# Shifting where the stationary operands of a 256-wide matmul stream lie in SBUF

## The chip, the core and the metric

One core of one Trainium2 chip runs the kernel. TensorE (PE) multiplies: an instruction first loads a stationary operand (LDWEIGHTS, the row PEld of the profile), then streams a moving operand through it into PSUM (MATMUL). VectorE is DVE, ScalarE is ACT, GpSimd is POOL, and SP issues DMAs. SBUF has 128 partitions; "byte" below means a byte within each partition. The metric is the device time of one execution, in microseconds (us).

## The reference

Linear attention with an RMS norm, followed by a feed-forward layer with GELU, all in fp32:

```
kv  = einsum('bhsd,bhse->bhde', k, v)            # q, k, v: 8 x 8 heads x 576 x 64
o   = einsum('bhsd,bhde->bhse', q, kv)
x   = o / sqrt(mean(o*o, -1) + 1e-6) * g_norm    # as 4608 tokens x 512
h   = x @ w_in                                   # 512 x 2048
out = gelu(h) @ w_out                            # 2048 x 512
```

## The kernel before

The 4608 tokens are handled in nine chunks of 512 (`CH`). Precision comes from splitting each fp32 operand into a high part in the fp32r format and the rest, so that one product is three matmuls: high by high, low by high, high by low. All work is recorded by hand in the order in which each engine runs it.

For the first two chunks (`PLAIN`) layer 1 is `layer1` (L529 in the profile): 128 x 128 weights stationary, 512 tokens streaming. Meanwhile the weights are loaded, split, and combined by `combine`, `high_sums` and `low_sums` into seven block sums per pair of feature blocks, written to DRAM as `products`.

For the last seven chunks layer 1 runs as a Strassen-like scheme, `layer1_pair` (L436): each of eight pairs of feature blocks takes seven products of six matmuls, 42 in all, with 256 columns streaming. The chunk has eight such pairs, so there are 7 x 8 x 42 = 2352 of these matmuls. Their stationary operand is a 128 x 128 piece (512 bytes) of a **ring** of four tiles, `w_in0` to `w_in3`, which `load_products` fills from DRAM (L419), one tile of 4096 bytes per two products, and refills as soon as its second product is issued. Their moving operand is a kilobyte of a token tile (`x0` to `x5` or `w_in5` to `w_in12`, by `piece_tile`). DVE adds (L446, L428) join the products in PSUM; ACT takes the GELU (L541, L542), DVE the low part (L547).

After each group of 42 comes layer 2, `layer2` (L555): 24 matmuls of 512 columns, with `gh`/`gl` or the tiles `w_in13`, `w_in14` stationary and `w_out` tiles moving. Between the two, now and then, stands `project` (L211): `q` times the key-value sums of the next chunk, six matmuls whose widths add up to 512 per part (a chunk of tokens may cross a batch). Its stationary operand is a 512-byte piece of `kv_h` or `kv_l`, its moving operand a piece of `qh`, `ql` or `w_in4`.

Tiles of the pool `const` lie one behind the other in SBUF in the order in which their names first occur; a name keeps its place, and the tile is used again under it. Four small constants come first, then `kv_h`, `kv_l`, `ident`, `fold`, `warm` (512 bytes of zeros for the matmuls of `keep_warm`, L638, early on), `half_g`, `heads`, and then the 4096-byte tiles.

Of the kernel before, what the change touches and what calls it, by code (L numbers as in the profile page):

```python
# [8 lines left out]
F32 = mybir.dt.float32  # L9
F32R = mybir.dt.float32r  # L10
I32 = mybir.dt.int32
# [5 lines left out]
P = 128  # L17
# [6 lines left out]
RING = 4  # L24
# [11 lines left out]
def linear_attn_rms_gelu_ffn(  # L36
# [18 lines left out]
    NT, DM = out.shape  # L55
# [5 lines left out]
    NF = w_in.shape[0]  # L61
# [4 lines left out]
    const = ctx.enter_context(tc.tile_pool(name="const", bufs=1))  # L66
# [8 lines left out]
    kv_l = [const.tile([P, NP, P], F32R, name=f"kv_l{s}") for s in range(2)]  # L75
    ident = const.tile([P, P], F32, name="ident")
    fold = const.tile([P, P], F32, name="fold")
    warm = const.tile([P, P], F32, name="warm")
    half_g = const.tile([P, 1], F32, name="half_g")
    heads = const.tile([P, 2], F32, name="heads")  # L80


    kv_in, late = {}, {}

    def late_tile(name):

        if name not in late:
            late[name] = const.tile([P, 2 * DM], I32, name=name).bitcast(F32)
        return late[name]
# [254 lines left out]
    kept = {}  # L344

    def reused(i, dtype=F32):

        if i not in kept:
            kept[i] = const.tile([P, 2 * DM], dtype, name=f"w_in{i}")
        return kept[i]  # L350

    def piece_tile(c, n):
        k = (["x2", "x3"] + [f"w_in{i}" for i in range(5, 10)],
# [40 lines left out]
    def high_sums():  # L394

        for (j, second), s in stage.items():
            if j % 2:
                t = reused(second, F32R).rearrange("p (k a n) -> p k a n", k=2, a=2)
            else:
                t = const.tile([P, 2, 2, HALF], F32R, name=f"x{2 + second}")  # L400
            nc.scalar.copy(out=t[:, :, 0], in_=s)
            halved[j, second] = s, t
        stage.clear()
# [10 lines left out]
    ring = {}  # L414

    def load_products(t):
        if t < (NCH - PLAIN) * NT2:
            ring[t] = reused(t % RING, F32R)
            nc.sync.dma_start(out=ring[t].bitcast(F32), in_=products[t % NT2])  # L419

    def layer1_pair(at, j, between):


        a, b = (ps_h.tile([P, CH], F32, name="ps_h") for _ in range(2))
        left, right = slice(0, HALF), slice(HALF, CH)
        u = reused(15).rearrange("p (a n) -> p a n", n=HALF)
        p1, u2, v, u3 = (u[:, i] for i in range(4))
        add = lambda out, x, y: nc.vector.tensor_tensor(out=out, in0=x, in1=y, op=ALU.add)  # L428

        def product(k, out, first=False):  # L430
            n = ((at.c - PLAIN) * NF // 2 + j) * NPR + k
            w, x = ring[n // 2][:, n % 2 * DM:(n % 2 + 1) * DM], at.x[k]
            for kb in range(2):
                hi, lo = (w[:, m * HALF + kb * P:m * HALF + (kb + 1) * P] for m in range(2))
                for i, (y, z) in enumerate(((hi, 0), (lo, 0), (hi, 1))):
                    nc.tensor.matmul(  # L436
                        out=out, lhsT=y, rhs=x[:, z, kb], start=first and kb + i == 0,
                        stop=kb == 1 and i == 2, skip_group_check=True,
                    )
            if n % 2:  # L440
                load_products(n // 2 + RING)
# [25 lines left out]
    raw, parts = {}, {}  # L467

    def load_w(n):
        kind, i = weights[n]  # L470
        src = w_in[i] if kind == "in" else w_out[i * P:(i + 1) * P, :]
        raw[n] = const.tile([P, 2 * DM], I32, name=f"w_{kind}{i}")
        nc.sync.dma_start(out=raw[n], in_=src.bitcast(I32))

    zs, ws = {}, {}
# [27 lines left out]

    def high_w(n):
        kind, i = weights[n]
        t = const.tile([P, 2 * DM], F32R, name=f"w_{kind}{i}")
        parts[kind, i] = t
        nc.scalar.copy(out=t[:, HI], in_=ws[n].bitcast(F32))

# [89 lines left out]

    attn = [Attn(c) for c in range(NCH)]  # L600
    first, second = attn[:2]
    nc.vector.memset(warm, 0.0)
    nc.scalar.activation(out=heads, in_=warm[:, :2], func=AF.Gelu)
    mask, g_row = late_tile(f"w_in{NF - 6}")[:, :P], late_tile(f"w_in{NF - 6}")[:1, P:2 * P]
# [12 lines left out]
    for h in range(2):  # L617
        nc.scalar.dma_start(out=g_row[:, h * D:(h + 1) * D], in_=g_norm.unsqueeze(0))
    load_w(0)
    for p in range(2):  # L620
        load_kv(1, p)
    for n in (1, 2, 3):
        load_w(n)
    for p in (2, 3):
        load_kv(1, p)
    load_w(4)
    second.load(0)
    for n in range(5, 9):
# [49 lines left out]
    n = 2 * NB  # L678
# [156 lines left out]
    def later(c, i):  # L835

        if i == 9:
            sums[c] = attn[c + 1].fold()
        if i in (5, 7):
            load_kv(c + 2, (i - 5) // 2)  # L840
        if i == 9:
            attn[c + 2].load(0)
        if i == 13:
            for p in (2, 3):
                load_kv(c + 2, p)
        if i == 15:
            attn[c + 2].load(1)
        if i == 13:
            for t in range(RING):
                load_products(t)  # L850
# [5 lines left out]
    def convert(i, gelu_rest, between):  # L856

        count = 3 if i in (2, 4, 6, 8) else 2 if i < 11 else i in (11, 12, 14)  # L860
        now = [order.pop(0) for _ in range(count)]
        for k, n in enumerate(now or [None]):
            if last:
                high_w(last[0])
                if last[0] + 2 < len(weights):
                    top_w(last[0] + 2)
            if not i and not k:
                gelu_rest()
                low_w(last.pop())
            if n is not None:  # L870
                bits_w(n)
            if i and not k:
                gelu_rest()
            if last:
                low_w(last.pop())
            if n is not None:
                last.append(n)
            if not k:
                between()
# [7 lines left out]
    for s in range(PLAIN * NF):  # L887
        c, i = divmod(s, NF)
# [7 lines left out]
        if c == 0:  # L896
# [4 lines left out]
            def between():  # L901
                if i == 0:
                    for p in (2, 3):
                        attn[0].low_x(p, nc.vector)
                if i in (9, 10):
                    high_w(i - 9)
                    low_w(i - 9)
                if i == 1:
                    split_kv(1, range(NP))
                    nc.scalar.copy(out=kv_h[0], in_=kv_f)  # L910
                    nc.vector.tensor_tensor(
                        out=kv_l[0], in0=kv_f, in1=kv_h[0].bitcast(F32), op=ALU.subtract
                    )
                spread_work(c, i)
# [9 lines left out]
        else:  # L924
# [3 lines left out]
            n = 0 if not 1 <= i <= 11 else 2 if i in (1, 3, 5, 7, 11) else 1  # L928
# [114 lines left out]
```

## Time and profile before

| | |
|---|---|
| three timed runs | 836.03, 837.2, 839.48 us; median 837.2 |
| the profiled execution | 835.6 us, of which 833.8 us are the span from first to last instruction |
| granted TensorE clock, mean | 0.999 |
| DVE, ACT, POOL busy | 59%, 38%, 8% of the span |
| TensorE rows of the first layer's products (L436) | 1392 + 960 matmuls, 283 ns each as reported |
| a ring load, issue to landing | least 3.1, median 4.6, most 9.2 us |

A reported matmul duration is from start to a modelled end, and neighbours overlap. What a matmul costs in a dense stream is the distance from its start to the next one's start, and this is read from the timeline, where the rows show starts.

### The profile page before, as it was taken

Reading aid. Unit: us, or ns where it says so; the run is one execution under the profiler, and the core shown is the slowest. Engines: PE = TensorE matmul, PEld = TensorE weight load, DVE = VectorE, ACT = ScalarE, POOL = GpSimd, SP = SyncE. Lnnn points to the kernel's source line nnn. Section 1 sums busy time; section 2 is a strip of 40 time slices with the busy share of each in tenths; the row PEclk is TensorE's granted clock in tenths of the full one; section 3 lists DMA queues with packets and bytes.
Section 4 is the critical chain, followed back from the end, with each engine's and each line's share of the span. In section 5 each row is a group of like instructions: output and inputs, shape, how many; then the busy total and the mean of one; then the engine's idle time right before and its main releaser. Section 6 shows DMA issues by size and latency. Waiting matters only on the chain.

```text
span 833.8 us, 13801 instructions
## 1 busy us (share of the span) xinstructions
PE 828.9 (99%) x5386; PEld 735.0 (88%) x5386; DVE 495.9 (59%) x980; ACT 314.2 (38%) x578; POOL 65.5 (8%) x69
## 2 busy tenths in 40 slices
PE   9999999999999999999999999999999999999998
PEld 7688888888999999999999999999999989999997
DVE  3999838687546744674457545673467446744443
ACT  3788444434532334233423253233323332322221
POOL 1000021011000101010001010010101000100000
PEclk9999999999999999999999999999999999999999
DMA  9981347776784568455945587456555655556551
GB/s 348 407 330 51 114 135 250 254 245 240 252 304 135 180 230 307 161 177 202 339 159 176 199 281 262 151 177 229 172 172 172 232 188 177 177 177 227 177 177 51
DMA packets 61605, 174.97 MB, mean 210 GB/s; under 512 B 6500, under 2 KB 15460, under 8 KB 61540
## 3 DMA queue, kind: packets, MB, share of 16 engines
q1 hardware_dynamic: 61536, 174.09, 60.0%
q8 instruction: 43, 0.70, 0.3%
q14 instruction: 22, 0.18, 0.1%
q10 hardware_dynamic: 4, 0.00, 0.0%
HBM read 149.95 MB, written 24.12 MB: 209 GB/s over the span
## 4 chain that ended last, share of the span: by engine, by line
PE 99%; DVE 0%; issue 0%; ACT 0%; DVEq 0%
PE acc L555 47%; PE ps_h L436 34%; PE ps_h L529 10%; PE ps_a L211 3%; PE ps_a L151 2%; PE ps_h L521 1%; PE ps_h L638 1%; PE acc L672 0%; PE acc L739 0%; PE ps_h L683 0%; PE ps_a L241 0%; DVE w L594 0%; DVE w_in L664 0%; PE ps_h L691 0%; DVE sq L583 0%
## 5 line engine op out<-in xcount | busy, mean ns | idle before, releaser
L555 PE MATMUL acc<-w_out,gh 128*128 128x512 f32 x700 | 217.0, 391 | 0.0
L436 PE MATMUL ps_h<-w_in,w_in 128*128 128x256 f32 x1392 | 176.2, 283 | 0.0
L436 PEld LDWEIGHTS ps_h<-w_in,w_in 128*128 128x128 f32 x1392 | 171.1, 192 | 0.0
L555 PE MATMUL acc<-w_out,w_in 128*128 128x512 f32 x672 | 159.7, 392 | 0.0
L555 PEld LDWEIGHTS acc<-w_out,gh 128*128 128x128 f32 x700 | 129.3, 188 | 25.5
L555 PEld LDWEIGHTS acc<-w_out,w_in 128*128 128x128 f32 x672 | 124.0, 188 | 24.8
L555 PE MATMUL acc<-w_out,gl 128*128 128x512 f32 x350 | 136.3, 390 | 0.0
L541 ACT ACTIVATE gh<-ps_h 128x512 fp32r<-128x512 f32 x88 | 52.7, 599 | 212.6 <-DVE ps_h L428 155.4
L436 PEld LDWEIGHTS ps_h<-x,w_in 128*128 128x128 f32 x960 | 122.6, 191 | 4.4
L436 PE MATMUL ps_h<-x,w_in 128*128 128x256 f32 x960 | 123.9, 283 | 0.0
L541 ACT ACTIVATE w_in<-ps_h 128x512 fp32r<-128x512 f32 x56 | 33.6, 600 | 184.7 <-DVE ps_h L428 184.7
L446 DVE COPY w_in<-ps_h 128x256 f32<-128x256 f32 x56 | 23.8, 425 | 133.1 <-PE ps_h L436 133.1
L428 DVE TENSOR_TENSOR ps_h<-ps_h,w_in 128x256 f32<-128x256 f32 x168 | 72.7, 432 | 48.0 <-PE ps_h L436 43.6
L428 DVE TENSOR_TENSOR w_in<-ps_h,w_in 128x256 f32<-128x256 f32 x168 | 71.4, 425 | 49.2 <-PE ps_h L436 47.2
L529 PE MATMUL ps_h<-x,w_in 128*128 128x512 f32 x360 | 86.8, 390 | 0.0
L547 DVE TENSOR_TENSOR gl<-ps_h,gh 128x512 fp32r<-128x512 f32 x88 | 60.4, 687 | 42.4 <-ACT ps_h L542 38.0
L542 ACT ACTIVATE ps_h<-ps_h 128x512 f32<-128x512 f32 x144 | 85.5, 594 | 0.0
L529 PEld LDWEIGHTS ps_h<-x,w_in 128*128 128x128 f32 x360 | 67.4, 188 | 13.9 <-POOL x L299 0.2
L555 PEld LDWEIGHTS acc<-w_out,gl 128*128 128x128 f32 x350 | 65.7, 188 | 14.1
L547 DVE TENSOR_TENSOR w_in<-ps_h,w_in 128x512 fp32r<-128x512 f32 x56 | 38.4, 686 | 17.1 <-ACT ps_h L542 17.1
L199 POOL TENSOR_TENSOR ql<-q,qh 128x512 fp32r<-128x512 f32 x16 | 21.1, 1321 | 211.5 <-ACT qh L198 140.9
L334 POOL TENSOR_TENSOR w_in<-o,w_in 128x512 fp32r<-128x512 f32 x13 | 16.9, 1325 | 210.8 <-ACT w_in L329 210.8
(153 smaller groups left out, 640.4 us busy)
## 6 DMA issues: line engine op xcount, KB each, us to landing
w_in<-products SPq DMA_DIRECT2D x196, 512.0 KB, 4.6
products<-w_in SPq DMA_DIRECT2D x40, 256.0 KB, 3.0
w_in<-w_in SPq DMA_DIRECT2D x16, 512.0 KB, 10.2
kv_main<-kv_main SPq DMA_DIRECT2D x16, 512.0 KB, 7.0
w_out<-w_out SPq DMA_DIRECT2D x16, 512.0 KB, 10.2
q<-qT SPq DMA_DIRECT2D x15, 512.0 KB, 5.7
out<-w SPq DMA_DIRECT2D x18, 256.0 KB, 2.1
out<-z SPq DMA_DIRECT2D x17, 256.0 KB, 2.3
```

Of the source, the lines that this page charges most:

```text
L151: nc.tensor.matmul(out=ps[r, n * D:(n + 1) * D], lhsT=k[:, r], rhs=v[:, r], start=(j == 0), stop=(j == NJ),)
L199: eng.tensor_tensor(out=ql, in0=q, in1=qh.bitcast(F32), op=ALU.subtract)
L211: nc.tensor.matmul(out=ps[:, a:e], lhsT=w, rhs=x[:, a:e], start=(m == 0), stop=(m == 2))
L334: eng.tensor_tensor(out=x[:, 1], in0=self.block(OPERANDS[n]), in1=x[:, 0].bitcast(F32), op=ALU.subtract,)
L428: add = lambda out, x, y: nc.vector.tensor_tensor(out=out, in0=x, in1=y, op=ALU.add)
L436: nc.tensor.matmul(out=out, lhsT=y, rhs=x[:, z, kb], start=first and kb + i == 0, stop=kb == 1 and i == 2, skip_group_check=True,)
L446: nc.vector.tensor_copy(out=p1, in_=a[:, left])
L529: nc.tensor.matmul(out=h, lhsT=parts["in", i][:, w][:, p * P:(p + 1) * P], rhs=at.x[p][:, x], start=(m + p == 0), stop=(m == 2 and p == NP ...
L541: nc.scalar.activation(out=gh, in_=h, func=AF.Gelu)
L542: nc.scalar.activation(out=h, in_=h, func=AF.Gelu)
L547: nc.vector.tensor_tensor(out=gl, in0=h, in1=gh.bitcast(F32), op=ALU.subtract)
L555: nc.tensor.matmul(out=ps, lhsT=x[:, ts], rhs=parts["out", i][:, w], start=(i == 0 and m == 0), stop=(m == 2 and (i == NF - 1 or (i, t) == ...
```

## The change

Each of the ring's four tiles `w_in0` to `w_in3` gets 64 elements (256 bytes) more, and the ring's loads and matmuls use the part that starts 48 elements (192 bytes) into the tile. Other uses of the same four tiles (the raw weights and their split parts early on, the staging tiles of `high_sums`) still start at the tile's first byte. To make room, `warm` is no longer a tile: it becomes a part of `w_in10`, which already holds other early constants.

```diff
-    warm = const.tile([P, P], F32, name="warm")
+    AWAY, ROOM = 48, 64
+
+    def block_tile(name, dtype):
+        ring = name in [f"w_in{i}" for i in range(RING)]
+        return const.tile([P, 2 * DM + (ROOM if ring else 0)], dtype, name=name)
...
-            kept[i] = const.tile([P, 2 * DM], dtype, name=f"w_in{i}")
-        return kept[i]
+            kept[i] = block_tile(f"w_in{i}", dtype)
+        return kept[i][:, :2 * DM]
...
-            ring[t] = reused(t % RING, F32R)
+            reused(t % RING, F32R)
+            ring[t] = kept[t % RING][:, AWAY:AWAY + 2 * DM]
...
-        raw[n] = const.tile([P, 2 * DM], I32, name=f"w_{kind}{i}")
+        raw[n] = block_tile(f"w_{kind}{i}", I32)[:, :2 * DM]
...
-        t = const.tile([P, 2 * DM], F32R, name=f"w_{kind}{i}")
+        t = block_tile(f"w_{kind}{i}", F32R)[:, :2 * DM]
...
+    warm = late_tile(f"w_in{NF - 6}")[:, DM + P:DM + 2 * P]
     nc.vector.memset(warm, 0.0)
```

Where the operands lie follows from the built program. The table gives the first byte of some tiles in a partition, and in brackets how far that is past a multiple of 256. Pieces within a tile start at multiples of 512 from it.

| tile | used as | before | after |
|---|---|---|---|
| `kv_h`, `kv_l` (four tiles) | stationary, L211 | 16512 to 22656 (128) | the same |
| ring part in `w_in0` | stationary, L436 | 59072 (192) | 58752 (128) |
| ring part in `w_in1` | stationary, L436 | 63168 (192) | 63104 (128) |
| ring part in `w_in2` | stationary, L436 | 71360 (192) | 71552 (128) |
| ring part in `w_in3` | stationary, L436 | 91840 (192) | 92288 (128) |
| `w_in5` | moving, L436 | 108224 (192) | 108736 (192) |
| `x2` | moving, L436 | 165568 (192) | 166080 (192) |
| `qh`, `ql` | moving, L211 | 198592, 200640 (192) | 199104, 201152 (192) |
| `gh` | stationary, L555 | 202688 (192) | 203200 (192) |
| `w_out2` | moving, L555 | 95936 (192) | 96448 (192) |

No other tile's remainder by 256 changes either, apart from the small `half_g` and `heads`. The order of the instructions is the same on every engine. One wait is new. On SP the rows around the load of `w_in10`, the tile in which `warm` now lies, were these (names carry buffer numbers; in brackets, what the instruction waits for):

```order
L473 DMA w_in_188<-w_in 128x1024 [waits DMAHW6_49]
L473 DMA w_out_190<-w_out 128x1024 [waits DMAHW7_49]
L473 DMA w_in_192<-w_in 128x1024 [waits DVE_49,DMAHW0_49,Activation_49,Pool_49]
L473 DMA w_out_194<-w_out 128x1024 [waits DMAHW1_49]
L473 DMA w_in_196<-w_in 128x1024 [waits DMAHW2_49,DVE_49,PE_49]
```

and are now these:

```order
L481 DMA w_in_187<-w_in 128x1024 [waits DMAHW6_49]
L481 DMA w_out_189<-w_out 128x1024 [waits DMAHW7_49]
L481 DMA w_in_191<-w_in 128x1024 [waits DVE_49,PE_49,DMAHW0_49,Activation_49,Pool_49]
L481 DMA w_out_193<-w_out 128x1024 [waits DMAHW1_49]
L481 DMA w_in_195<-w_in 128x1024 [waits DMAHW2_49,DVE_49,PE_49]
```

The load of `w_in10` (the third row) now waits for TensorE as well, since the early matmuls on zeros read that tile.

## The prediction

> **What bounds the kernel now.** I read the page first: busy shares, then the chain that ended last.
>
> ```profile
> PE 828.9 (99%) x5386; PEld 735.0 (88%) x5386; DVE 495.9 (59%) x980; ACT 314.2 (38%) x578; POOL 65.5 (8%) x69
> PEclk9999999999999999999999999999999999999999
> PE acc L555 47%; PE ps_h L436 34%; PE ps_h L529 10%; PE ps_a L211 3%; PE ps_a L151 2%; PE ps_h L521 1%; PE ps_h L638 1%; PE acc L672 0%; PE acc L739 0%; PE ps_h L683 0%; PE ps_a L241 0%; DVE w L594 0%; DVE w_in L664 0%; PE ps_h L691 0%; DVE sq L583 0%
> ```
>
> TensorE is busy from end to end, the clock is granted in full, and the chain is TensorE alone. The first layer's products (L436), whose stationary operand is what the change moves, hold 34% of 833.8 us, some 283 us. The view of who waited for whom, taken for PE, is two rows long:
>
> ```profile
> PE ps_h L638 <- DVE warm L602: 1.1, 1, 1.1
> PE acc L672 <- DVE w_in L664: 0.6, 2, 0.4
> ```
>
> Both are at the start. So there is no stall to remove: the change can only act on the distance from one matmul's start to the next. The page's duration of a matmul (283 ns) doesn't give that, because neighbours overlap; the timeline of PE does. It gives start, length, and how many:
>
> ```profile
> 302.30 0.39 PE L555 MATMUL acc<-w_out,gl 128*128 128x512 f32 x1
> ...
> 307.07 0.39 PE L555 MATMUL acc<-w_out,gl 128*128 128x512 f32 x1
> 307.29 3.04 PE L436 MATMUL ps_h<-x,w_in 128*128 128x256 f32 x24
> 310.17 2.32 PE L436 MATMUL ps_h<-w_in,w_in 128*128 128x256 f32 x18
> 312.33 0.28 PE L211 MATMUL ps_a<-w_in,kv_h 128*128 128x256 f32 x1
> ```
>
> Read the starts. From 307.29 to 310.17 are 24 products, from 310.17 to 312.33 are 18: 2.88/24 = 2.16/18 = **120.0 ns each**. From 302.30 to 307.07 are 21 matmuls of layer 2 (they come in threes): 4.77/21 = 227.1 ns each. Twice the columns cost 107 ns more, so about 0.42 ns is a column's time, and 120 ns is 107 ns of streaming and 13 ns of something else; 227 ns leaves the same 13 or 14 ns. The products have 2352 x 13 ns = 31 us of this. That is all there is to win, and one nanosecond per product is 2.35 us.
>
> **Does the place of the operands bear on these 13 ns?** Before, stationary and moving pieces of L436, L529 and L555 all start 192 bytes past a multiple of 256. `project` (L211) is the only stream of the same kind in which they differ: `kv` lies 128 past, `q` 192 past. That is exactly how the change places the products. In one chunk `project` is 256 columns wide, the same shape as the products:
>
> ```profile
> 301.15 0.28 PE L211 MATMUL ps_a<-qh,kv_h 128*128 128x256 f32 x1
> 301.26 0.28 PE L211 MATMUL ps_a<-qh,kv_l 128*128 128x256 f32 x1
> 301.37 0.28 PE L211 MATMUL ps_a<-ql,kv_h 128*128 128x256 f32 x1
> 301.49 0.28 PE L211 MATMUL ps_a<-qh,kv_h 128*128 128x256 f32 x1
> 301.60 0.28 PE L211 MATMUL ps_a<-qh,kv_l 128*128 128x256 f32 x1
> 301.71 0.28 PE L211 MATMUL ps_a<-ql,kv_h 128*128 128x256 f32 x1
> 301.83 0.63 PE L555 MATMUL acc<-w_out,gh 128*128 128x512 f32 x2
> ...
> 315.75 0.28 PE L211 MATMUL ps_a<-qh,kv_h 128*128 128x256 f32 x1
> ...
> 316.46 2.89 PE L555 MATMUL acc<-w_out,w_in 128*128 128x512 f32 x12
> 319.19 1.00 PE L436 MATMUL ps_h<-x,w_in 128*128 128x256 f32 x7
> ```
>
> At 301.15, right behind a group of products, six take 0.68 us: **113 ns each**, and every step is 110 or 120 ns in rows rounded to 10. At 315.75, right behind layer 2, six take 0.71 us: **118 ns**. Both are below 120.0, with the same opcode, shape, data type and clock. (Rounding leaves 2 ns either way on a mean of six, so 118 could nearly be 120; 113 could not.) Wider ones of the same stream show nothing of the sort:
>
> ```profile
> 682.03 0.39 PE L211 MATMUL ps_a<-w_in,kv_h 128*128 128x512 f32 x1
> 682.26 0.39 PE L211 MATMUL ps_a<-w_in,kv_l 128*128 128x512 f32 x1
> 682.49 0.39 PE L211 MATMUL ps_a<-w_in,kv_h 128*128 128x512 f32 x1
> 682.72 0.62 PE L555 MATMUL acc<-w_out,gh 128*128 128x512 f32 x2
> ```
>
> Three of 512 columns take 0.69 us, 230 ns each against 227 in layer 2: no gain, rather a loss of 3 ns. So the reading is narrow: with 256 columns a weight load lies beside the whole of the matmul before it, and there the place of the two operands seems to matter; with 512 it doesn't.
>
> **The change part by part.**
>
> *The shift of the ring.* After it all 2352 products have the placing of the L211 rows. The size per product is between 120.0 − 113.3 = 6.7 ns and −3 ns (the 512-wide rows). Which row is nearest? The products always follow layer 2, and the 256-wide row that follows layer 2 is the one at 315.75, with 118.3 ns. I take it: (120.0 − 118.3) x 2352 = 1.7 x 2352 = 4.0 us. That it is one group of six, and that the stream's pace depended on what ran ahead of it, are why I keep the other ends.
>
> *Leaving the stream.* Behind a group of products or of fast `project` matmuls, layer 2 needs a little longer than its own pace; the next rows show it behind another 256-wide `project` that follows products (six in 0.68 us again).
>
> ```profile
> 324.22 0.28 PE L211 MATMUL ps_a<-w_in,kv_h 128*128 128x256 f32 x1
> ...
> 324.90 0.63 PE L555 MATMUL acc<-w_out,gh 128*128 128x512 f32 x2
> ...
> 330.37 3.04 PE L436 MATMUL ps_h<-x,w_in 128*128 128x256 f32 x24
> ```
>
> 24 take 5.47 us, 20 ns more than 24 x 227.1; behind the 118 ns group, 12 take 2.73 us (316.46 to 319.19), 5 ns more than 12 x 227.1. With 56 groups of products, some 15 ns each come back: 0.8 us, say 1. Sum: 5 us.
>
> *The longer tiles.* Everything behind the ring moves by multiples of 256 bytes; layer 2's operands keep their remainders, and its 24 matmuls after each group kept the same 227 ns whether their stationary was `gh` or `w_in` (2.73/12 above is 227.5 as well), though these lie a different number of kilobytes from `w_out`. I take nothing, and bound it by 1 ns on 1722 matmuls of layer 2, 1.7 us either way.
>
> *The ring's loads* land on other bytes, as many as before.
>
> ```profile
> w_in<-products SPq DMA_DIRECT2D x196, 512.0 KB, 4.6
> DMA to landing us min/median/max: 3.1/4.6/9.2
> ```
>
> A tile is refilled while the three others serve 36 products, and a layer 2 always falls into that stretch: 36 x 0.120 + 5.45 = 9.8 us against a landing of 4.6 us (9.2 at most). Products at 113 ns leave 9.5. Cost nothing; if the cover were gone, a load late by 1 us in a few of 196 places would cost a few microseconds, and PE's waits show none now.
>
> *The faster PE* asks DVE for its sums sooner:
>
> ```profile
> 308.93 0.42 DVE L446 COPY w_in<-ps_h 128x256 f32<-128x256 f32 x1 [3.70 <-PE ps_h L436]
> 310.37 0.42 DVE L428 TENSOR_TENSOR w_in<-ps_h,w_in 128x256 f32<-128x256 f32 x1 [0.56 <-PE ps_h L436]
> ```
>
> The copy is done at 309.35, and the product that writes there again starts at 310.17; at 113 ns this slack of 0.8 us shrinks by less than 0.1. Nothing is late next: TensorE's stream is still the longest.
>
> *`warm` inside `w_in10`.* The memset, the same matmuls and the same waits. The load of `w_in10` on SP now waits for TensorE too; behind it on SP stand the other weight loads.
>
> ```profile
> 38.91 0.33 SPq L473 DMA_DIRECT2D w_in<-w_in  x1
> L638 PEld LDWEIGHTS ps_h<-warm x26: 186/333/338, 1.1 to 18.3; 128*128 128x128 f32 x26
> ```
>
> The load is issued at 38.91 us; the last matmul on zeros starts at 18.4. The wait is over 20 us before: nothing.
>
> Against the profiled execution: 835.6 − 5 = 830.6 us. The median shown is 1.6 us above that execution, so 837.2 − 5 = **832.2 us**, a ratio of 0.994.
>
> **The rivals.**
>
> *A, the full step.* The stream settles at the pace of the rows at 301.15 (113.3 ns). For: the groups at 301.15 and 324.22, both behind products, hold it for six matmuls each, the first without drifting, and 42 in a row have time to settle. Against: the only group that starts behind layer 2 as the products do held 118. Price: 6.7 x 2352 = 15.7 us; **821.5 us**.
>
> *B, no effect.* The 113 and 118 ns come from something else in `project` (its place in the stream, PSUM tile or the region where `kv` lies), and the products stay at 120 ns: **837 us**. For: the 512-wide rows gain nothing from the same placing. Against: the 42 products from 307.29 on read four ring tiles and seven token tiles in many places, always at the same remainder, and their pace is 120.0 throughout. The Trainium skill, "TensorE: Matmul & The Clock Gate", section "Part 2: What happens when you issue a matmul", says that loading the next tile's weights takes no SBUF read bandwidth from the running matmul, since the two have ports of their own; by it no address could matter and B would hold. The rows at 301.15 speak against it, though no run yet shows that the address is the reason.
>
> *C, slower.* The placing hurts where it is not accompanied by `project`'s own order: the products behave as the 512-wide `project` rows, 3.3 ns longer than streams at equal remainders. That is 3.3 x 2352 = 7.8 us; **845 us**. It decides from 1.8 ns per product on (4.2 us). Against: those rows are 512 wide, the products are not.
>
> **How the numbers follow.** My forecast (118, allowing 115.5 to 119.5) has 0.42, A (113 to 115.5) 0.28, B 0.20, C 0.10. The forecast is the likeliest, so 832.2 us. The range takes in A and B with the bound of layer 2: from 821.5 − 1 = 820.5 to 837.2 + 1.7 = 839; it leaves out most of C. Measurements of this kernel can tell a change of about 0.5%, 4.2 us. Faster by more: all of A and about three quarters of my own case, 0.60. Within: the rest of it and B, and a little of C: 0.32. Slower by more: 0.08.
>
> **What would show it.** In the timeline of the changed kernel, the 24 first products of a group behind layer 2: 2.84 us if 118, 2.72 if A, 2.88 if B, 2.96 if C. L555 stays at 227 ns, L529 as it is, PE's list of waits stays two rows, and 34% of the chain falls to about 33%. I'd be wrong if the pace depends on something that `project` has and the products don't, or if layer 2 changes its pace although its remainders are the same.

## The result, and the profile after

The changed kernel took 830.35 us (median of four runs, 829.81 to 831.25) against 838.34 us of the kernel before beside it (836.03 to 841.06): a ratio of 0.9916, 95% interval 0.989 to 0.9941. Measured once more on another occasion (e12 below) it took 830.14 us against 836.1, a ratio of 0.9924 (0.9901 to 0.9947). The forecast was 832.2 us and a ratio of 0.994.

The profiled execution of the changed kernel took 831.25 us, its span 829.5. First the page's busy shares and its chain by line (line numbers are 7 to 9 higher now: L444 is what L436 was, L563 is L555, L218 is L211):

```profile
PE 824.6 (99%) x5386; PEld 731.4 (88%) x5386; DVE 496.3 (60%) x980; ACT 314.0 (38%) x578; POOL 65.7 (8%) x69
PEclk9999999999999999999999999999999999999999
PE acc L563 47%; PE ps_h L444 33%; PE ps_h L537 10%; PE ps_a L218 3%; PE ps_a L158 3%; PE ps_h L529 1%; PE ps_h L647 1%; PE acc L681 1%; PE acc L748 0%; PE ps_h L692 0%; PE ps_a L248 0%; DVE w L602 0%; DVE w_in L673 0%; PE ps_h L700 0%; DVE sq L591 0%
```

TensorE still holds the whole chain, and the products went from 34% to 33% of it. The view of who waited for whom on PE still has two rows, both at the start:

```profile
PE ps_h L647 <- DVE w_in L611: 1.1, 1, 1.1
PE acc L681 <- DVE w_in L673: 0.6, 2, 0.4
```

So nothing new waits on TensorE, and the ring's loads land as they did (median 4.6, most 9.0 us). The timeline of PE shows the same group of products as before, and the `project` groups around it; the first column is the start:

```profile
302.14 0.63 PE L563 MATMUL acc<-w_out,gh 128*128 128x512 f32 x2
...
307.59 2.99 PE L444 MATMUL ps_h<-x,w_in 128*128 128x256 f32 x24
310.41 2.28 PE L444 MATMUL ps_h<-w_in,w_in 128*128 128x256 f32 x18
312.53 0.28 PE L218 MATMUL ps_a<-w_in,kv_h 128*128 128x256 f32 x1
...
313.24 2.89 PE L563 MATMUL acc<-w_out,w_in 128*128 128x512 f32 x12
```

From 307.59 to 312.53 are 42 products in 4.94 us, where it was 5.04: 117.6 ns each in place of 120.0. The 24 matmuls of layer 2 ahead of them take 5.45 us, 227.1 ns each, as before. And `project` behind the products (312.53 to 313.24) now takes 0.71 us for its six where it took 0.68, although the distance of its own operands is what it was: behind products at the same distance it goes on at their pace. All distances between starts added up, the 2352 products took 276.9 us in place of 281.8, and layer 2 took 393.2 in place of 393.9. That is 5.6 us. The two profiled spans differ by 4.3 us only: all other matmuls together took 1.3 us more in this execution, whose granted clock was 0.95 over its first 33 us (1.00 in the kernel before). What the medians differ by beyond 5.6 us, 6 to 8 us in all, lies within the scatter of the kernel before, whose runs reach from 835 to 841 us.

### The profile page after: what moved, and what is told of

Read it like the earlier page. It is cut to its first block, busy times and chain, and to the rows that moved or that the text cites. A ratio compares the mean times of both kernels' runs of the same rounds, so it can differ in the third digit from the quotient of the medians.

```text
span 829.5 us, 13801 instructions
## 1 busy us (share of the span) xinstructions
PE 824.6 (99%) x5386; PEld 731.4 (88%) x5386; DVE 496.3 (60%) x980; ACT 314.0 (38%) x578; POOL 65.7 (8%) x69
## 4 chain that ended last, share of the span: by engine, by line
PE 99%; DVE 0%; issue 0%; ACT 0%; DVEq 0%
PE acc L563 47%; PE ps_h L444 33%; PE ps_h L537 10%; PE ps_a L218 3%; PE ps_a L158 3%; PE ps_h L529 1%; PE ps_h L647 1%; PE acc L681 1%; PE acc L748 0%; PE ps_h L692 0%; PE ps_a L248 0%; DVE w L602 0%; DVE w_in L673 0%; PE ps_h L700 0%; DVE sq L591 0%
## 5 line engine op out<-in xcount | busy, mean ns | idle before, releaser
L563 PE MATMUL acc<-w_out,gh 128*128 128x512 f32 x700 | 216.7, 391 | 0.0
L444 PE MATMUL ps_h<-w_in,w_in 128*128 128x256 f32 x1392 | 173.0, 279 | 0.0
L444 PEld LDWEIGHTS ps_h<-w_in,w_in 128*128 128x128 f32 x1392 | 167.8, 188 | 0.0
L563 PE MATMUL acc<-w_out,w_in 128*128 128x512 f32 x672 | 159.3, 391 | 0.0
L563 PEld LDWEIGHTS acc<-w_out,gh 128*128 128x128 f32 x700 | 129.2, 188 | 25.3
L563 PEld LDWEIGHTS acc<-w_out,w_in 128*128 128x128 f32 x672 | 123.9, 188 | 24.6
L563 PE MATMUL acc<-w_out,gl 128*128 128x512 f32 x350 | 136.3, 389 | 0.0
L444 PEld LDWEIGHTS ps_h<-x,w_in 128*128 128x128 f32 x960 | 120.9, 188 | 4.3
L444 PE MATMUL ps_h<-x,w_in 128*128 128x256 f32 x960 | 122.2, 279 | 0.0
L436 DVE TENSOR_TENSOR ps_h<-ps_h,w_in 128x256 f32<-128x256 f32 x168 | 72.7, 433 | 46.1 <-PE ps_h L444 42.3
L436 DVE TENSOR_TENSOR w_in<-ps_h,w_in 128x256 f32<-128x256 f32 x168 | 71.4, 425 | 46.8 <-PE ps_h L444 44.9
L555 DVE TENSOR_TENSOR gl<-ps_h,gh 128x512 fp32r<-128x512 f32 x88 | 60.4, 687 | 43.0 <-ACT ps_h L550 38.7
L563 PEld LDWEIGHTS acc<-w_out,gl 128*128 128x128 f32 x350 | 65.7, 188 | 13.9
L555 DVE TENSOR_TENSOR w_in<-ps_h,w_in 128x512 fp32r<-128x512 f32 x56 | 38.4, 686 | 17.1 <-ACT ps_h L550 17.1
```

The costliest lines, as they stand in the source:

```text
L444: nc.tensor.matmul(out=out, lhsT=y, rhs=x[:, z, kb], start=first and kb + i == 0, stop=kb == 1 and i == 2, skip_group_check=True,)
L555: nc.vector.tensor_tensor(out=gl, in0=h, in1=gh.bitcast(F32), op=ALU.subtract)
L563: nc.tensor.matmul(out=ps, lhsT=x[:, ts], rhs=parts["out", i][:, w], start=(i == 0 and m == 0), stop=(m == 2 and (i == NF - 1 or (i, t) == ...
```

## The experiments

"Distance" below is the start of the stationary operand less that of the moving one, by its remainder in steps of 256 bytes: 0 before the change, 192 after it. Every kernel computes the whole result. A pace "from the starts" is the mean distance between the starts of neighbouring matmuls in the trace, taken by place in the group of 42; where rows can show it, they do.

### The longer tiles alone, and other shifts: e1, e2, e3

```diff
-    AWAY, ROOM = 48, 64
+    AWAY, ROOM = 0, 64      # e1; 16 in e2, 32 in e3
```

Expected of e1:

> The changed kernel with the ring's operands put back at the tiles' first byte: the longer tiles and the moved zeros stay, the shift of 192 bytes goes. Theory R (what counts is where the stationary operand lies relative to the moving one): the products are back at 120.0 ns each, 2.88 us for the 24 behind a layer 2, and the time is that of before within 0.5%. Rival G (the longer tiles or the removed tile made the gain): the products stay at 118 ns and the time stays near 830 us.

Of e2:

> The changed kernel with the shift at 64 bytes in place of 192, so that the ring's operands start at a multiple of 256, 64 bytes past the moving ones' remainder. Theory R doesn't say what 64 bytes give: 120 ns if the two streams still meet, 113 to 118 if any distance helps. Rival L (the weight load itself is faster when it starts at a multiple of 128 bytes, wherever the moving operand is): 118 ns, as with 192 bytes.

Of e3:

> The changed kernel with the shift at 128 bytes: the ring's operands start 64 bytes past a multiple of 256. Rival L (alignment of the weight load to 128 bytes): 120 ns, since the start is again 64 past a multiple of 128, as before the change. Theory R: some pace other than 120 ns is possible, 113 to 118, since the distance to the moving operand is 128.

Measured: e1 836.5 us, ratio 1.0005 (0.999 to 1.002); e2 832.26 us, 0.9945 (0.9927 to 0.9963); e3 837.71 us, 1.0021 (1.0006 to 1.0036). The timeline of PE, e1:

```profile
307.49 3.04 PE L444 MATMUL ps_h<-x,w_in 128*128 128x256 f32 x24
310.37 2.32 PE L444 MATMUL ps_h<-w_in,w_in 128*128 128x256 f32 x18
312.53 0.28 PE L218 MATMUL ps_a<-w_in,kv_h 128*128 128x256 f32 x1
```

e2:

```profile
308.15 2.99 PE L444 MATMUL ps_h<-x,w_in 128*128 128x256 f32 x24
310.98 2.29 PE L444 MATMUL ps_h<-w_in,w_in 128*128 128x256 f32 x18
313.10 0.28 PE L218 MATMUL ps_a<-w_in,kv_h 128*128 128x256 f32 x1
```

e3:

```profile
307.77 3.05 PE L444 MATMUL ps_h<-x,w_in 128*128 128x256 f32 x24
310.66 2.32 PE L444 MATMUL ps_h<-w_in,w_in 128*128 128x256 f32 x18
312.82 0.28 PE L218 MATMUL ps_a<-w_in,kv_h 128*128 128x256 f32 x1
```

42 products take 5.04 us in e1, 4.95 in e2, 5.05 in e3: 120.0, 117.9 and 120.2 ns. So the longer tiles and the moved zeros do nothing (to within 0.2%), and the shift does all of it. In e1 the ring tiles also lie elsewhere against the token tiles than in the kernel before, `w_in1` by 768 bytes, and the pace is the same 120.0: steps of 256 bytes do nothing, which is why the distance is counted by its remainder. Shifts of 64 and 192 bytes give the same pace, 0 and 128 nearly the same (e3's products took 282.7 us from the starts, against 281.8). These three kernels don't decide between theory R and rival L: starts 64 bytes past a multiple of 128 are the slow ones (the kernel before, e1, e3), starts at a multiple of 128 the fast ones (the changed kernel, e2), just as L has it. The next kernel separates the two.

### Everything moved together: e4

```diff
     heads = const.tile([P, 2], F32, name="heads")
+    pad = const.tile([P, 48], F32, name="pad")
```

> The kernel before with an unused tile of 192 bytes ahead of the large tiles, so that the ring's operands and the moving operands all start 128 bytes past a multiple of 256. Rival L (alignment of the weight load alone): the products fall to 118 ns. Theory R: the two are at the same remainder again, so the products stay at 120.0 ns; and the 256-wide products of q with the key-value sums, whose stationary operand keeps its 128 and whose moving one now has 128 too, rise from 113 and 118 to 120 ns.

One execution, 836.45 us beside a median of 836.84 for the kernel before. Its timeline of PE (L437 are the products, L212 is `project`):

```profile
307.67 3.04 PE L437 MATMUL ps_h<-x,w_in 128*128 128x256 f32 x24
310.54 2.32 PE L437 MATMUL ps_h<-w_in,w_in 128*128 128x256 f32 x18
312.70 0.28 PE L212 MATMUL ps_a<-w_in,kv_h 128*128 128x256 f32 x1
...
313.42 2.91 PE L556 MATMUL acc<-w_out,w_in 128*128 128x512 f32 x12
316.17 0.28 PE L212 MATMUL ps_a<-qh,kv_h 128*128 128x256 f32 x1
...
316.88 2.91 PE L556 MATMUL acc<-w_out,w_in 128*128 128x512 f32 x12
```

The stationary operands start where the changed kernel has them, 128 past a multiple of 256, and the products are at 120 ns (18 in 2.16 us). `project`, at distance 0 for the first time, takes 0.72 us for six behind the products, 120 ns where it was 113. With the stationary operands of both streams at remainder 128, the pace is 120 ns: at these places it is the distance between the two operands that counts, not the start of the stationary one.

One part of the expectation failed. The group of `project` behind layer 2 (316.17 to 316.88) takes 0.71 us at distance 0, just as it did at distance 192, and not 0.72. The starts show why: its steps are 113, 119 and then four of 120 ns, in sum 712; at distance 192, in the kernel before, they were 118, 118, 118, 117, 118 and 115, in sum 704. The first products of each group in the kernel before also go at 113.3, 119.1 and then 120.0 ns. Six matmuls behind layer 2 are too few to tell the two distances apart in rows rounded to 10 ns.

### Finer steps, four distances in one kernel: e5, e8

```diff
-    AWAY, ROOM = 48, 64
+    AWAY, ROOM = (8, 24, 40, 56), 64      # e5; (2, 4, 12, 52) in e8
...
-            ring[t] = kept[t % RING][:, AWAY:AWAY + 2 * DM]
+            ring[t] = kept[t % RING][:, AWAY[t % RING]:AWAY[t % RING] + 2 * DM]
```

> The changed kernel with a shift of its own for each ring tile: 32, 96, 160 and 224 bytes for w_in0 to w_in3. So far 0 and 128 bytes gave 120 ns per product, 64 and 192 gave 117.8. Theory S (steps of 64 bytes count, and what lies between goes with its neighbours): 32, 96, 160 and 224 each give between 117 and 121 ns, the same for all four, since each lies halfway. Theory T (the distance counts byte by byte and the streams meet only near 0 and 128): all four below 118.5 ns, and one of them may be at the 113 ns that the products of q held right behind products at distance 0. A tile serves twelve products in a row, so each pace is read from steps 3 to 12.

> The changed kernel with 8, 16, 48 and 208 bytes of shift for w_in0 to w_in3. Theory S (steps of 64 bytes): 8 and 16 still at 120 ns, 48 near 118, 208 at 118. Theory T (byte by byte): 8 and 16 already differ from 120 ns.

From the starts, means over the 588 products of each tile: e5 118.5, 118.6, 119.6 and 116.8 ns for 32, 96, 160 and 224 bytes; e8 116.4, 118.2, 118.3 and 116.7 ns for 8, 16, 48 and 208. Steps of 64 bytes (S) are out: 8 bytes already make a difference. That all lie below 118.5 (T) is out too: 160 bytes give 119.6. Single steps from start to start range from 112 to 125 ns within a tile, and the same place in a chunk's eight groups gives the same value to about a nanosecond in every chunk. The times of one execution each, 836.68 and 833.46 us, aren't read further: in e5 the products took 3.5 us less than before, but all other matmuls together 4.4 us more, with a granted clock of 0.90 over the first 33 us (1.00 in the kernel before).

### What runs ahead: e6 and its mirror, e11

`load_products` places each product of a tile by itself: 192 bytes in, or at distance 0 where it is the first of its group of seven.

```diff
-            ring[t] = kept[t % RING][:, AWAY:AWAY + 2 * DM]
-            nc.sync.dma_start(out=ring[t].bitcast(F32), in_=products[t % NT2])
+            at = [AWAY + DM * a if (2 * t + a) % NPR else 0 + (DM + ROOM) * a for a in range(2)]
+            ring[t] = [kept[t % RING][:, o:o + DM] for o in at]
...
-            w, x = ring[n // 2][:, n % 2 * DM:(n % 2 + 1) * DM], at.x[k]
+            w, x = ring[n // 2][n % 2], at.x[k]
```

(A tile whose halves no longer touch is loaded by two DMAs. In e11 the condition picks the last product of the group, `!= NPR - 1`.)

> The changed kernel with the first product of each group of seven (six matmuls) at distance 0 again and the other six at 192 bytes; its tile is loaded by two DMAs in place of one. In the trace of before, matmuls at 192 bytes ran at 113 ns right behind a stream at distance 0 and at 118 ns right behind layer 2. Theory M (the pace is set by how the stream is entered, and holds): the first product runs at 113, 119, 120 ns, then the other 36 at 113.3, 4.8 us per group in place of 4.95; with 56 groups some 6 to 9 us less than the changed kernel, about 822 to 825 us. Rival D (the 113 ns decay within some ten matmuls): the last products of a group are at 118, and the time is within 2 us of the changed kernel's 830.

> As the kernel with the first product of each group at distance 0, but it is the last product that is at 0; the tiles are loaded with as many DMAs. Theory M (the pace is set by how the stream is entered): the first six products are at 118 ns as in the changed kernel, the last one near 120, and the time is that of the changed kernel within 2 us, about 830. Rival Q (one product in seven at another distance, or the split loads, make the 113 ns): the six products at 192 bytes run at 113 ns here too, and the time is near 822 us.

e6 took **822.47 us**, a ratio of 0.9826 (0.9802 to 0.985) to the kernel before. Its timeline of PE:

```profile
305.69 2.92 PE L454 MATMUL ps_h<-x,w_in 128*128 128x256 f32 x24
308.45 2.20 PE L454 MATMUL ps_h<-w_in,w_in 128*128 128x256 f32 x18
310.49 0.28 PE L218 MATMUL ps_a<-w_in,kv_h 128*128 128x256 f32 x1
```

The 18 products from 308.45 on take 2.04 us: 113.3 ns each. From the starts, over all 56 groups, the first product's six go at 113.3, 119.1, 120.0, 120.0, 120.0 and 120.9 ns, and each of the next 36 at 113.3 or 113.4. The products take 268.4 us in all. e11 (one execution, 831.37 us), the same number of loads and of shifted products, only the odd one last:

```profile
306.91 2.99 PE L454 MATMUL ps_h<-x,w_in 128*128 128x256 f32 x24
309.74 2.28 PE L454 MATMUL ps_h<-w_in,w_in 128*128 128x256 f32 x18
311.86 0.28 PE L218 MATMUL ps_a<-w_in,kv_h 128*128 128x256 f32 x1
```

24 in 2.83 us, 118 ns, for operands that run at 113 ns in e6. So distance 192 has two paces, each steady over 36 matmuls, and what ran ahead decides which. I missed the last product: it stays at 118.2 ns on the mean from the starts, not near 120. Distance 0, entered from products at 192 bytes, doesn't reach 120 within six.

### Layer 2: e7

```diff
+        if p == 3:
+            work.tile([P, 48], F32, name="pad")
         sq[p] = work.tile([P, CH], F32, name=SQ[p], bufs=2 if p == 3 else None)
```

> The kernel before with an unused tile of 192 bytes ahead of gh, so that the stationary operands of those layer 2 products that use gh and gl lie 192 bytes from the moving ones' remainder, while those that use w_in13 and w_in14 stay at distance 0; the first layer's products are as before. If the gain were a matter of the two operands' distance alone, the 512-wide products would fall from 227 to some 224 ns, 1050 of them, 2 to 3 us. As I read the 512-wide products of q (229 to 230 ns), they gain nothing: 227 to 230 ns, and the time is that of before or up to 3 us more.

838.2 us, a ratio of 1.0022 (1.0005 to 1.0039). The timeline of PE:

```profile
303.06 0.39 PE L555 MATMUL acc<-w_out,gl 128*128 128x512 f32 x1
...
307.87 0.39 PE L555 MATMUL acc<-w_out,gl 128*128 128x512 f32 x1
308.10 3.04 PE L436 MATMUL ps_h<-x,w_in 128*128 128x256 f32 x24
...
313.14 0.28 PE L211 MATMUL ps_a<-w_in,kv_h 128*128 128x256 f32 x1
...
313.85 2.93 PE L555 MATMUL acc<-w_out,w_in 128*128 128x512 f32 x12
...
320.05 3.04 PE L436 MATMUL ps_h<-x,w_in 128*128 128x256 f32 x24
...
325.08 0.28 PE L211 MATMUL ps_a<-w_in,kv_h 128*128 128x256 f32 x1
...
325.76 0.62 PE L555 MATMUL acc<-w_out,gh 128*128 128x512 f32 x2
```

21 matmuls of 512 columns at distance 192 take 4.81 us, 229.0 ns, against 227.1 at distance 0. The shift that helps 256 columns costs these 512-wide ones 2 ns; all of layer 2 took 395.4 us from the starts, 1.5 us more than before.

The rows behind them show how far back the stream's history reaches. The 42 products from 308.10 on follow a layer 2 at distance 192, those from 320.05 on one at distance 0 (its stationary tiles are `w_in13` and `w_in14`). Both groups are at distance 0 and take 5.04 and 5.03 us. But `project` behind the first takes 0.71 us for its six (313.14 to 313.85), behind the second 0.68 (325.08 to 325.76), with the same distance and the same width; in the kernel before all three such groups take 0.68. From the starts, the products of the first kind settle into a cycle of five (122.9, 118.3, 118.3, 120.6, 120.0 ns, on the mean 120.0), those of the second at 120.0 each. So what ran ahead of a stream can still show behind 42 matmuls of the same mean pace.

### Other uniform distances, and the change again: e9, e10, e12

```diff
-    AWAY, ROOM = 48, 64
+    AWAY, ROOM = 2, 64      # e9; 56 in e10
```

> The changed kernel with a shift of 8 bytes for all four ring tiles. With tiles at four distances in one kernel, the one at 8 bytes ran at 115 to 117 ns, but each tile ran behind another distance. If the pace belongs to the distance, all products are at 115 to 116 ns and the products take some 271 us, 5 to 6 less than with 192 bytes: about 825 us. If it belongs to the entry (as the run with the first product at zero says), 8 bytes entered from layer 2 may settle elsewhere, at 118 to 120 ns: 830 to 836 us.

> The changed kernel with a shift of 224 bytes for all four ring tiles. In the mixed kernel the tile at 224 bytes ran at 113.9 to 119.3 ns, 116.8 on the mean. If the pace belongs to the distance: about 117 ns per product. If to the entry: anything between 113 and 120 ns, the same in every group, since every group is entered from layer 2.

> The changed kernel itself once more, for its ratio beside the others on one chip: 0.992 to 0.995 of the kernel before. Its products took 4.9 us less in the trace, its layer 2 0.7 us less; if that is all, the ratio is 0.993 to 0.994; the first measurement's 0.9916 would then be partly scatter of the kernel before.

e9 took 825.5 us, a ratio of 0.9866 (0.9837 to 0.9895):

```profile
305.48 2.94 PE L444 MATMUL ps_h<-x,w_in 128*128 128x256 f32 x24
308.26 2.25 PE L444 MATMUL ps_h<-w_in,w_in 128*128 128x256 f32 x18
310.35 0.28 PE L218 MATMUL ps_a<-w_in,kv_h 128*128 128x256 f32 x1
```

Its 24 take 2.78 us, its 18 take 2.09: 116 ns, from the starts 116.7, 115.0, 115.0 in turn once four matmuls have passed, and 272.4 us for all products. Entered from layer 2 like the changed kernel, it is 4.6 us faster than that (830.14 us beside it). e10, one execution, 832.03 us: 116.7 ns on the mean, in a cycle of four (115.8, 117.5, 120.0, 113.3 ns) that is the same in every group. So the distance sets the pace as well as the entry does; e12 is told of at the top.

## Why the prediction was right, point by point

- **The bound.** TensorE alone, no waits to remove: it held, the list of waits has the same two rows.
- **Products at 118 ns.** Forecast 118.3 from the one `project` group that starts behind layer 2, measured 117.6 in the rows (117.7 from all starts). Choosing that row, and not the ones at 113 ns, was the step that carried the number. Its reason was right: e6 and e11 show that the entry decides between 113 and 118.
- **Luck in that reading.** The row holds six matmuls and was set against 120.0, the pace of whole groups. The first six products of a group in the kernel before, behind layer 2 too but at distance 0, take 712 ns from the starts; the six of the row take 704. In rows both are 0.71 us, so this row could not show that the distance matters; e4's group at distance 0 reads the same 0.71. The row that did show it is the one at 301.15, with 113 ns. Only the starts separate 118 from 120: from the third step on, products at distance 0 hold 120.0, and the row has 118, 117, 118 and 115.
- **The size.** 1.7 ns per product were forecast. Once settled, 2.3 came (120.0 to 117.7); over all products it is 2.1, because before the change the first two of each group took only 113.3 and 119.1. That makes 4.9 us where the sum had 4.0.
- **Leaving the stream.** Forecast about 1 us back in layer 2; measured 0.7 us over its 1722 matmuls. By place, from the starts, the first five behind the products take 17.6 ns less in all, in the 32 cases where no `project` lies between: 0.56 us of the 0.7.
- **The longer tiles, the moved zeros.** Nothing that can be told, by e1 (ratio 1.0005, 0.999 to 1.002), which has both without the shift.
- **Loads, DVE, the new wait.** No row of PE's waits names them.
- **512 columns gain nothing from such a distance.** Read from three 512-wide `project` rows with a loss of 3 ns; e7 found a loss of 2. The prediction also put it that with 512 columns the place of the two operands doesn't matter; by e7 it does, the other way.
- **Rival A (113 ns).** Not in the changed kernel. The reason that I gave for doubting it, that the pace depended on what ran ahead, is what e6 and e11 show; with another entry the price that I gave for A, 821.5 us, is nearly reached (822.47).
- **Rival B (no effect).** Fell with e1 beside the changed kernel. The rule that it leaned on, in the Trainium skill, "TensorE: Matmul & The Clock Gate", section "Part 2: What happens when you issue a matmul", is that weights and moving operand have read ports of their own, so that a weight load takes no SBUF read bandwidth from the running matmul. What the prediction drew from it, that no address could matter, does not hold here: moving the stationary operands alone by 192 bytes took 4.9 us off the 2352 products, 2.1 ns each, and e4, which moves both, took nothing off them. Whether read bandwidth is what they share, no run here shows.
- **Rival C (slower).** Not for 256 columns at 192 bytes; e3 (128 bytes, ratio 1.0021) and e7 (512 columns, 1.0022) are mild cases of it.

What stays open is why. The runs show that the distance of the two operands matters down to 8 bytes, that 64 and 192 give the same pace and 0 and 128 nearly so, that at 192 bytes a stream of 36 keeps the pace that it was entered with, and that at 192 bytes 512 columns lose about the 2 ns that 256 gain. A meeting of the two streams of reads somewhere on their way to the array would fit this, but it is not shown: no run tests it.

The fastest version here is e6, 8 us faster than the change. Whether the first product's 120 ns can be saved too, or a distance of 8 bytes be entered better, wasn't tried.

## What to carry to other kernels

Where TensorE is busy all the time and every matmul brings a new stationary operand, read its pace from the starts in the timeline, by shape and by what ran ahead, and compare streams of the same shape whose operands lie differently: a few nanoseconds per matmul are a per cent. Then try the distance between stationary and moving operands as a parameter, with one tile made a little longer and everything else kept at its remainder. What a group inside the kernel already does at that distance gave the best forecast here, since it was entered from the same stream. Compare such a group with equally many matmuls, counted from the same entry, and from the starts themselves: the first two matmuls behind another stream can be several nanoseconds off the pace that settles.

## What the runs showed of the hardware

- The same 256-wide matmuls, at full clock (1.00 over their stretch) and with no wait, ran at anything from 113.3 to 120.2 ns on the mean, by the operands' distance and by the stream ahead. The lowest steady pace was 113.3 ns (e6). The Trainium skill, "TensorE: Matmul & The Clock Gate", section "Back-to-back issue gap", gives 262 cycles at 2.4 GHz for an isolated one, by estimate 109 ns. With a weight load for each, no stream here came to it.
- The reported length of a weight load differs too, though it doesn't follow the pace. The profile of the instructions of one line gives least, median and most; before:

```profile
L436 PEld LDWEIGHTS ps_h<-w_in,w_in x1392: 192/192/192, 210.2 to 819.2; 128*128 128x128 f32 x199
```

and in the changed kernel:

```profile
L444 PEld LDWEIGHTS ps_h<-w_in,w_in x1392: 187/188/188, 211.3 to 814.9; 128*128 128x128 f32 x199
```

The median is 192 ns at distance 0 and 188 at distance 192: a hint, before any start is compared, that two streams differ. It is no measure of the pace: e3, with products at 120.2 ns, has 189, and e6, at 113.3, has 188 like the changed kernel.

- One product of six matmuls at another place, 0.7 us of the 10.4 us that a group and its layer 2 take, changed the pace of the 36 matmuls behind it by 4 ns each.
